# The third expert's first layer by seven half products, in the last three token pairs instead of the last two

## The chip, the cores and the metric

The kernel runs on one NeuronCore of one Trainium2 chip. The metric is the device time of one execution in microseconds (us). Shorter is better.

## The reference

An attention stage (4 batches, 8 heads, 768 positions, head width 64; three heads attend to the whole past, five to four sink positions and a window of 64) gives `x`, 3072 tokens of 512 values. A mixture of four experts then works on every token:

```python
p = domain_probs / (domain_probs.sum(-1, keepdims=True) + 1e-09)
out = zeros((N, D))                      # N = 3072, D = 512
for e in range(4):
    h = maximum(x @ w1[e], 0.0)          # w1[e]: 512 x 1024
    out += p[:, e:e+1] * (h @ w2[e])     # w2[e]: 1024 x 512
```

The change is in the product `x @ w1[e]` of one expert, for 256 of the 3072 tokens.

## The kernel before, in words

**Stages.** The tokens are cut in 24 tiles of 128. Tiles 0 to 3 are done in a plain way. Tiles 4 to 23 are done two at a time: ten *pairs*, whose first tiles are 4, 6, ..., 18, 20, 22 (`pairs`; `nt0` is the first tile of a pair, `nxt` that of the following one). The attention of the later tokens is woven into the earlier pairs and has ended before pair 18 begins. From there only the mixture is left.

**A pair** (`pair_steps`) is a first layer for four experts, then one second layer over all four. The probability is multiplied into the inputs beforehand (`scale_inputs`, L1150, on VectorE), so the second layer can sum over the experts in PSUM. The hidden values go to `hA`, five blocks of 16 x 128 columns: A11, A21, A12, A22 and `S1 = A21 + A22`.

**A plain first layer** (`plain_layer1`, L1199) is four steps of eight matmuls with 256 columns each. Every step fills one of four PSUM banks of the pool `pA`, and ScalarE empties it with a ReLU (L1208).

**A first layer by seven half products** (`winograd_layer1`, L1228) cuts weights and inputs in 2 x 2 blocks and makes seven products instead of eight, each of eight matmuls with 128 columns. Call them 1 to 7. They use two banks, x and y, that accumulate:

- 1 goes into x; ScalarE copies x out (`keep`, L1238).
- 2 goes into a `pA` bank; VectorE adds the copy and clips (`add`, L1245).
- 3 is accumulated on x, and x is copied out.
- 4 goes into y, and y is copied out.
- 5 is accumulated on x; VectorE adds a copy and clips.
- 6 is accumulated on y; VectorE adds a copy and clips.
- 7 is accumulated on x; ScalarE reads x with a ReLU (L1278).

It needs sums of inputs (`scaled_sums`, L1166 and two `minus` at L992, then one `minus` inside step 4) and sums of weights, made once per expert (`first_weight_sums`: three new matrices `more[0]` to `more[2]`, and `more[3]`, which overwrites a quarter of `w1sb`).

**Which expert goes which way.** Expert 3 (`EW[0]`; its steps are called `a`) goes by half products in all pairs. Expert 2 (`EW[1]`, `b`) does so from pair 18 on (`two`). Expert 1 (`EW3`, `third`) does so in pairs 20 and 22 (`three`). Expert 0 is always plain (`n`). Where all three run, `b` has two banks of the pool `pV` for itself, with its own copies in `kS`, and `a` and `third` use the two banks of `pO` one after the other. The weight sums of expert 1 go to `vS`, the attention's room for values.

**The second layer** (`product`, L1361) is seven products of 16 matmuls with 256 columns, on the two `pO` banks again (`x`, `y`), with VectorE making S2, S3 and S4 between them (L992) and adding (L1384), and ScalarE copying (L1381). Beside it VectorE scales the inputs of the next pair.

**Order.** The order of all engines' instructions is written out by hand: in `pair_steps`, `order` is a list of (steps of TensorE work with what empties their banks, an operation placed after them). An engine works through its own list strictly in that order.

Of the kernel before, what the change touches and what calls it, by code (L numbers as in the profile page):

```python
# [19 lines left out]
def kernel(  # L20
# [80 lines left out]
    def bank():  # L101
        return pA.tile([P, 512], FP32, name="pA", bufs=4)
# [11 lines left out]
    EW = (E - 1, E - 2)  # L114
# [229 lines left out]
    def w1_tile(e, ct, ft):  # L344

        return w_tile(e, w1sb[:, e * DMP + ct, :], ft)
# [208 lines left out]
    def mm_ns(cols):  # L555
        return cols / 2.4 + 2.5
# [434 lines left out]
    def minus(out, a, b):  # L991
        nc.vector.tensor_tensor(out=out, in0=a, in1=b, op=ALU.subtract)  # L992
# [15 lines left out]
    def first_weight_sums(e):  # L1008

        return [  # L1010
            lambda: minus(t1[e, 0], w1_part(e, 0, 1), w1_part(e, 0, 0)),
            lambda: minus(t1[e, 1], w1_part(e, 1, 1), t1[e, 0]),
            lambda: minus(t1[e, 2], w1_part(e, 1, 0), t1[e, 1]),
            lambda: minus(w1_part(e, 0, 1), w1_part(e, 1, 1), w1_part(e, 0, 1)),
        ]

    def room_for_more_sums():

        x = kR[0].rearrange("p c n t x -> p (c n t x)")
        y = att.tile([P, KH * FN], FP16, name="t1", tag="k_rows", bufs=1)  # L1020
        for n in range(3):
            z = x[:, n * KH * FN : (n + 1) * KH * FN] if n < 2 else y
            t1[EW[1], n] = z.rearrange("p (c f) -> p c f", c=KH)
        x = att.tile([P, DMP * PC], FP16, name="xs1", tag="q16", bufs=1)
        own_room[EW[1]] = x.rearrange("p (c x) -> p c x", c=DMP)

    EW3 = E - 3

    def room_for_third():

        n = KH * FN
        for i in range(3):
            t1[EW3, i] = vSf[:, i * n : (i + 1) * n].rearrange("p (c f) -> p c f", c=KH)
# [90 lines left out]
    def load_probs(nt0):  # L1124
        pB_of[nt0] = moe.tile([P, PT, E, P], FP32, name="pB", tag="pB", bufs=1)
        rows = p_rows[nt0 : nt0 + PT, :]
        nc.sync.dma_start(
            out=pB_of[nt0].rearrange("p t e x -> p (t e x)"),
            in_=bass.AP(rows.tensor, rows.offset, [[0, P], [1, PT * E * P]]),
        )  # L1130

    def scaled(e):
        if e in own_room:
            return own_room[e]
        n = 2 if e == EW[0] else e % 2
        x = xs_of[0][:, n * DMP * PC : (n + 1) * DMP * PC]
        return x.rearrange("p (c x) -> p c x", c=DMP)

    def scale_inputs(nt0, e):

        if xs_of[0] is None:
            xs_of[0] = moe.tile([P, XS], FP16, name="xs", tag="xs", bufs=1)
        xs = scaled(e)
        for g, c0, t0, n in pieces(nt0):
            require(g)
            xin = xT[g][:, :, c0 : c0 + n * P].rearrange("p c (t x) -> p c t x", t=n)
            o = xs[:, :, t0 * P : (t0 + n) * P].rearrange("p c (t x) -> p c t x", t=n)
            pb = pB_of[nt0][:, t0 : t0 + n, e, :]
            pb = pb.rearrange("p t (c x) -> p c t x", c=1)
            nc.vector.tensor_tensor(  # L1150
                out=o, in0=xin, in1=pb.to_broadcast([P, DMP, n, P]), op=ALU.mult
            )

    def x_part(e, i, j):
        return scaled(e)[:, j * KH : (j + 1) * KH, i * P : (i + 1) * P]
# [3 lines left out]
    def x_sum(e, n):  # L1159

        n0 = (2 * P * 8 if e in second_set else WT * NSH * P) + n * KH * P
        return kSf[:, n0 : n0 + KH * P].rearrange("p (c x) -> p c x", c=KH)

    def scaled_sums(e):

        nc.vector.tensor_tensor(  # L1166
            out=x_sum(e, 0), in0=x_part(e, 1, 0), in1=x_part(e, 1, 1), op=ALU.add
        )
        minus(x_sum(e, 1), x_sum(e, 0), x_part(e, 0, 0))
        minus(x_part(e, 1, 0), x_part(e, 0, 0), x_part(e, 1, 0))  # L1170

    def first_sum(e, n=1):
        k = slice(e * HT, (e + n) * HT)
        nc.vector.tensor_tensor(
            out=S1[:, k, :], in0=A21[:, k, :], in1=A22[:, k, :], op=ALU.add
        )
# [8 lines left out]
    def two(nt0):  # L1185
        return nt0 >= pairs[-LAST]

    def three(nt0):
        return nt0 >= pairs[-2]

    def pair_steps(nt0, nxt):

        def plain_layer1(e):
            xs = scaled(e)
            for f0 in range(0, FTP, 2):
                ps = bank()
                for f in range(2):
                    for ct in range(DMP):
                        nc.tensor.matmul(  # L1199
                            out=ps[:, f * PC : (f + 1) * PC],  # L1200
                            lhsT=w1_tile(e, ct, f0 + f),
                            rhs=xs[:, ct, :],
                            start=(ct == 0),
                            stop=(ct == DMP - 1),
                        )
                b0 = 2 * (f0 // HT)
                k0 = e * HT + f0 % HT
                nc.scalar.activation(  # L1208
                    out=blocks[:, b0 : b0 + 2, k0 : k0 + 2, :].rearrange(
                        "p t f x -> p f t x"  # L1210
                    ),
                    in_=ps.rearrange("p (f t x) -> p f t x", f=2, t=2),
                    func=AF.Relu,
                )
                yield 2 * DMP * mm_ns(PC), 0.5
# [69 lines left out]
        a, b = (winograd_layer1(e, *y) for e, y in zip(EW, (banks, banks[::-1])))  # L1285
        if three(nt0):
# [5 lines left out]
            b = winograd_layer1(EW[1], *more_banks, more_kept)  # L1292
            third = winograd_layer1(EW3, *banks)

        more, last_more = [], None
        if nt0 == pairs[-LAST - 2]:
            room_for_more_sums()
            more = first_weight_sums(EW[1])
        elif nt0 == pairs[-LAST - 1]:
            last_more = first_weight_sums(EW[1])[3]  # L1300
        elif nt0 == pairs[-3]:
            room_for_third()
            more = first_weight_sums(EW3)
            last_more = more[3]
        if not two(nt0):
            n = itertools.chain(*(plain_layer1(e) for e in range(E - 1)))
            order = (
                ((n,), lambda: scale_inputs(nt0, 1)),
                ((n,), more[0] if more else None),
                ((n, a), lambda: last_weight_sum(E - 1) if nt0 == pair0 else None),  # L1310
                ((n, a), None),
                ((n, a), lambda: scale_inputs(nt0, 2)),
                ((n, a), lambda: load_probs(nxt)),
                ((n, a), more[1] if more else None),
                ((n, a), more[2] if more else None),
                ((n, a), lambda: first_sum(0, 2)),
                ((n,), None),
                ((n, n), lambda: first_sum(2, 2)),
                ((), lambda: scale_inputs(nxt, 1) if two(nxt) else None),
            )  # L1320
        elif three(nt0):
            n = plain_layer1(0)
            order = (
                ((), lambda: scaled_sums(EW[1])),
                ((a, b, a, b), lambda: load_probs(nxt) if nxt else None),
                ((a, b, a, b), None),
                ((a, b, a, b), None),
                ((a, b), lambda: scaled_sums(EW3)),
                ((n,), None),
                ((third, third, n), lambda: first_sum(EW[0])),  # L1330
                ((third, third, n), lambda: first_sum(EW[1])),
                ((third, third, n), lambda: first_sum(0)),
                ((third,), lambda: first_sum(EW3)),
            )
        else:
            n = itertools.chain(plain_layer1(0), plain_layer1(1))
            order = (
                ((a, a, n), more[0] if more else None),
                ((a, a, n), lambda: load_probs(nxt) if nxt else None),
                ((a, a, n), more[1] if more else None),  # L1340
                ((n,), lambda: scaled_sums(EW[1])),
                ((a, b, n), more[2] if more else None),
                ((b, b, n), lambda: first_sum(0)),
                ((b, b, n), lambda: first_sum(EW[0])),
                ((b, n, b), lambda: (first_sum(1), first_sum(EW[1]))),
            )
        for steps, op in order:
            for x in steps:
# [56 lines left out]

        last = nxt is None
        ahead = nxt and two(nxt)
        if ahead and three(nxt):
            inputs_for_third()
        half = KT // 2 * mm_ns(HN), PSHARE  # L1410
        yield from product(x, A11, b(0, 0), True)
# [62 lines left out]
    pairs = list(range(pair0, NTILE, PT))  # L1474
# [145 lines left out]
```

The softmax here doesn't subtract the row's maximum and nothing guards it: scores larger than these inputs give would overflow.

## Time and profile before

| what | value |
|---|---|
| time, median of 3 runs | 376.77 us (376.42 to 377.32) |
| the profiled execution, its own time | 376.68 us |
| span of the profiled execution | 375.0 us |
| TensorE busy | 367.9 us (98%) |
| VectorE busy | 279.0 us (74%) |
| ScalarE busy | 227.4 us (61%) |
| clock granted to TensorE | full in all slices |

The span runs from the first to the last instruction. The time has 1.7 us around it. In the trace, pair 18 runs from 296.10 us to 321.56 us, pair 20 from 321.56 us to 346.66 us, and pair 22 after it. PE is TensorE's matmuls, PEld its weight loads, DVE VectorE, ACT ScalarE, POOL GpSimd, SP SyncE. A line such as L1228 is that of kernel.py.

### The profile page before, as it was taken

How to read it: one execution, taken by the hardware profiler on the slowest of the kernel's cores; microseconds unless marked ns; L12 is line 12 of the kernel's file. 1: busy time of each engine (PE TensorE's matmuls, PEld its weight loads, DVE VectorE, ACT ScalarE, POOL GpSimd, SP SyncE). 2: the span in 40 equal slices, each digit the busy share in tenths (PEclk: the TensorE clock that was granted, in tenths of full speed). 3: DMA queues.
4: the chain of work that ended last, by engine and by line, in shares of the span. 5: the costliest groups of instructions: out<-in, count | busy, mean ns of one | idle time of the engine just before them, and what ended most of it. 6: DMA issues, size and time to landing. Idle time of an engine off the chain costs nothing.

```text
span 375.0 us, 10225 instructions
## 1 busy us (share of the span) xinstructions
PE 367.9 (98%) x4176; PEld 311.1 (83%) x4176; DVE 279.0 (74%) x599; ACT 227.4 (61%) x475; POOL 113.3 (30%) x155
## 2 busy tenths in 40 slices
PE   8899999999999999999999999999999999999996
PEld 5755466668998988999989898998899998998996
DVE  7774768697788669868658858957767968969762
ACT  3863478547785785765676955784778362450630
POOL 8924673982058038115601650320000000000000
PEclk9999999999999999999999999999999999999999
DMA  8999999999699569977904990951220300300101
GB/s 161 155 204 208 195 189 192 186 207 100 97 109 149 101 94 116 163 112 56 207 14 60 171 159 14 133 127 14 67 73 3 98 18 0 114 2 2 58 3 56
DMA packets 123747, 39.24 MB, mean 105 GB/s; under 512 B 113728, under 2 KB 116356, under 8 KB 123700
## 3 DMA queue, kind: packets, MB, share of 16 engines
q0 software_dynamic: 85824, 19.01, 58.7%
q1 hardware_dynamic: 36276, 19.18, 21.8%
q8 instruction: 32, 0.52, 0.6%
q10 hardware_dynamic: 1600, 0.39, 0.5%
q14 instruction: 15, 0.12, 0.1%
HBM read 44.89 MB, written 6.34 MB: 137 GB/s over the span
## 4 chain that ended last, share of the span: by engine, by line
PE 95%; DVE 2%; ACT 2%; issue 0%; ACTq 0%
PE pO L1361 31%; PE pA L1199 23%; PE pO L1228 9%; PE pA L1065 7%; PE pO L1086 7%; PE pA L678 5%; PE pV L734 2%; PE pV L806 2%; PE pA L1228 2%; PE pV L1228 1%; PE pO L448 1%; PE pA L576 1%; ACT es L696 1%; DVE xs L1150 1%; PE pA L1453 0%; ACT rc L824 0%
## 5 line engine op out<-in xcount | busy, mean ns | idle before, releaser
L1361 PEld LDWEIGHTS <-hA 128*128 128x128 f16 x1104 | 104.9, 98 | 12.3
L1199 PE MATMUL pA<-xs,w1sb 128*128 128x256 f16 x800 | 101.3, 273 | 0.0
L1199 PEld LDWEIGHTS <-w1sb 128*128 128x128 f16 x800 | 74.7, 98 | 7.9
L1208 ACT ACTIVATE hA<-pA 128x512 f16<-128x512 f32 x100 | 59.6, 598 | 31.2 <-PE pA L1199 29.0
L1361 PE MATMUL pO<-w2sb,hA 128*128 128x256 f16 x640 | 76.7, 272 | 0.0
L696 ACT ACTIVATE es<-pA 128x384 f16<-128x384 f32 (+2 forms) x122 | 59.2, 511 | 26.9 <-PE pA L678 23.0
L306 POOL DMA_DIRECT2D vS<-in_v_dram x30 | 29.6, 987 | 112.0 <-PE pV L806 111.0
L1361 PE MATMUL pO<-tsb,hA 128*128 128x256 f16 x464 | 56.7, 272 | 0.0
L1150 DVE TENSOR_TENSOR xs<-xT,pB 128x1024 f16<-128x1024 f16 (+1 forms) x49 | 47.0, 977 | 0.0
L992 DVE TENSOR_TENSOR hA<-hA 128x1024 f16<-128x1024 f16 x60 | 39.5, 685 | 0.5
L1078 ACT ACTIVATE hA<-pA 128x384 f16<-128x384 f32 (+1 forms) x64 | 22.2, 385 | 19.4 <-PE pA L1065 19.2
L1065 PE MATMUL pA<-xT,w1sb 128*128 128x384 f16 (+1 forms) x256 | 30.9, 273 | 0.8 <-DMA w1sb<-in_moe_w_dram 0.5
L1086 PE MATMUL pO<-w2sb,hA 128*128 128x512 f16 x128 | 30.7, 379 | 0.0
L1228 PEld LDWEIGHTS <-w1sb 128*128 128x128 f16 x480 | 29.6, 98 | 1.2 <-issue 0.2
L829 DVE TENSOR_TENSOR xT<-pV,rc 64x384 f16<-64x384 f32 x37 | 20.5, 554 | 11.8 <-ACT rc L834 9.4
L1381 ACT COPY s<-pO 128x256 f32<-128x256 f32 x31 | 11.5, 373 | 27.7 <-PE pO L1361 21.9
L1065 PEld LDWEIGHTS <-w1sb 128*128 128x128 f16 x256 | 19.4, 98 | 9.7 <-issue 1.4
L824 ACT ACTIVATE rc<-pV,eps 64x384 f32<-64x384 f32 x37 | 21.3, 576 | 6.5 <-PE pV L806 5.9
L700 DVE TENSOR_TENSOR es<-es,mS 128x384 f16<-128x384 f16 (+1 forms) x40 | 13.7, 344 | 15.0 <-ACT es L696 15.0
L1245 DVE CUSTOM_DVE_ANT_0 hA<-pO,s 128x512 f16<-128x512 f32 x26 | 17.6, 688 | 9.7 <-PE pO L1228 8.3
L1238 ACT COPY s<-pO 128x512 f32<-128x512 f32 x39 | 22.5, 587 | 2.3 <-PE pO L1228 2.0
L678 PE MATMUL pA<-qT,kR 128*128 128x384 f16 (+2 forms) x120 | 22.9, 278 | 0.4 <-DVE kR L595 0.2
(163 smaller groups left out, 515.6 us busy)
## 6 DMA issues: line engine op xcount, KB each, us to landing
pB<-p_rows SPq DMA_DIRECT2D x10, 512.0 KB
out_dram<-o SPq DMA_DIRECT2D x19, 256.0 KB
w1sb<-in_moe_w_dram POOLq DMA_DIRECT2D x8, 512.0 KB, 9.1
w2sb<-in_moe_w_dram POOLq DMA_DIRECT2D x4, 1024.0 KB, 12.4
vS<-in_v_dram POOLq DMA_DIRECT2D x30, 112.0 KB, 4.3
k_rows<-in_k_dram POOLq DMA_DIRECT2D x18, 128.0 KB, 5.5
q<-in_q_dram POOLq DMA_DIRECT2D x18, 128.0 KB, 7.0
vR<-in_v_dram POOLq DMA_DIRECT2D x24, 48.0 KB, 5.8
```

Of the source, the lines that this page charges most:

```text
L306: gp.dma_start(out=t[:, :, own_v(h)], in_=windows_of(v, b, h, c))
L678: nc.tensor.matmul(out=ps[:, o : o + nq], lhsT=key_tile(b, c, h, t), rhs=qTs[b, c][:, hp, q0 : q0 + nq], start=(n == 0 or not first), stop ...
L696: nc.scalar.activation(out=es[:, 0:cols], in_=ps[:, 0:cols], func=AF.Exp, scale=SC)
L992: nc.vector.tensor_tensor(out=out, in0=a, in1=b, op=ALU.subtract)
L1065: nc.tensor.matmul(out=pss[ft][:, 0:cols_n], lhsT=w1_tile(e, ct, ft), rhs=x[:, ct, :], start=(n == 0), stop=(n == DMP - 1),)
L1086: nc.tensor.matmul(out=ps_o, lhsT=hs[:, ft, j * P : (j + 1) * P], rhs=w2sb[:, e * FTP + ft, :], start=(ft == 0), stop=(ft == FTP - 1),)
L1150: nc.vector.tensor_tensor(out=o, in0=xin, in1=pb.to_broadcast([P, DMP, n, P]), op=ALU.mult)
L1199: nc.tensor.matmul(out=ps[:, f * PC : (f + 1) * PC], lhsT=w1_tile(e, ct, f0 + f), rhs=xs[:, ct, :], start=(ct == 0), stop=(ct == DMP - 1),)
L1208: nc.scalar.activation(out=blocks[:, b0 : b0 + 2, k0 : k0 + 2, :].rearrange("p t f x -> p f t x"), in_=ps.rearrange("p (f t x) -> p f t x" ...
L1228: nc.tensor.matmul(out=ps[:, f * P : (f + 1) * P], lhsT=w_tile(e, w[:, ct, :], f), rhs=a[:, ct, :], start=(first and f == 0 and ct == 0), ...
L1238: nc.scalar.copy(out=kept[n], in_=ps)
L1361: nc.tensor.matmul(out=ps, lhsT=a[:, k, :], rhs=b(k), start=(first and k == 0), stop=(k == KT - 1), skip_group_check=not first,)
```

## The change

In pair 18 expert 1 is done by seven half products too, in place of four plain steps. Its weight sums, which pair 18 made for the pairs after it, are now all made within pair 18's first layer; `more[3]` moves there from the end of the pair. Pair 18 takes over the arrangement of pairs 20 and 22 (`b` on `pV`, `third` on `pO` after `a`), with an order of its own.

```diff
     def three(nt0):
-        return nt0 >= pairs[-2]
+        return nt0 >= pairs[-3]
...
         elif nt0 == pairs[-3]:
             room_for_third()
             more = first_weight_sums(EW3)
-            last_more = more[3]
...
+        elif nt0 == pairs[-3]:
+            n = plain_layer1(0)
+            order = (
+                ((a, a, n), lambda: scaled_sums(EW[1])),
+                ((b, b, n), more[0]),
+                ((a, b, a, b), more[1]),
+                ((a, b, a, b), more[2]),
+                ((n, a, b), lambda: (scaled_sums(EW3), load_probs(nxt))),
+                ((third, third, n), more[3]),
+                ((third, third), lambda: first_sum(EW[0])),
+                ((third, third), lambda: first_sum(EW[1])),
+                ((third,), lambda: (first_sum(0), first_sum(EW3))),
+            )
         elif three(nt0):
             n = plain_layer1(0)
             order = (
...
                 ((third, third, n), lambda: first_sum(EW[0])),
                 ((third, third, n), lambda: first_sum(EW[1])),
                 ((third, third, n), lambda: first_sum(0)),
                 ((third,), lambda: first_sum(EW3)),
             )
-        else:
-            n = itertools.chain(plain_layer1(0), plain_layer1(1))
-            order = (
-                ((a, a, n), more[0] if more else None),
-                ((a, a, n), lambda: load_probs(nxt) if nxt else None),
-                ((a, a, n), more[1] if more else None),
-                ((n,), lambda: scaled_sums(EW[1])),
-                ((a, b, n), more[2] if more else None),
-                ((b, b, n), lambda: first_sum(0)),
-                ((b, b, n), lambda: first_sum(EW[0])),
-                ((b, n, b), lambda: (first_sum(1), first_sum(EW[1]))),
-            )
...
-        if ahead and three(nxt):
+        if ahead and three(nt0):
             inputs_for_third()
```

The last edit keeps `inputs_for_third` where it was: at the second layers of pairs 18 and 20.

## The prediction

> **What bounds the kernel now.** I read the busy table first, then the chain that ended last, then the stage of the change.
>
> ```profile
> PE 367.9 (98%) x4176; PEld 311.1 (83%) x4176; DVE 279.0 (74%) x599; ACT 227.4 (61%) x475; POOL 113.3 (30%) x155
> ...
> PE 95%; DVE 2%; ACT 2%; issue 0%; ACTq 0%
> ```
>
> TensorE is the bound: 98% busy, and 95% of the chain. What counts is matmul time and any gap that opens between matmuls. The view of busy time by stage, for the two layers of pair 18 and of pair 20, shows no gap there at all (the first PE number is busy time, to be held against the length before it):
>
> ```profile
> 296.10:309.34 13.24, 13.24 (x178) 12.51 (x177) 9.21 (x18) 8.38 (x16) 0.00 (x0) 1.00 0.28 82
> 309.34:321.56 12.22, 12.22 (x115) 10.96 (x113) 10.56 (x22) 1.96 (x5) 0.00 (x0) 1.00 0.01 1
> 321.56:334.44 12.88, 12.88 (x203) 12.51 (x201) 9.60 (x23) 8.08 (x16) 0.00 (x0) 1.00 0.25 83
> ```
>
> Pair 20's first layer already does what pair 18's is to do, and takes 12.88 us against 13.24. But it does so in another order. How its last half products are spaced is seen in the timeline of PE (start, length, what):
>
> ```profile
> 326.92 0.61 PE L1228 MATMUL pO<-xs,t1sb 128*128 128x128 f16 x8
> 327.37 0.61 PE L1228 MATMUL pV<-xs,t 128*128 128x128 f16 x8
> 327.82 1.04 PE L1199 MATMUL pA<-xs,w1sb 128*128 128x256 f16 x8
> 328.69 0.61 PE L1228 MATMUL pO<-vS,w1sb 128*128 128x128 f16 x8
> ...
> 330.46 1.06 PE L1228 MATMUL pO<-kS,vS 128*128 128x128 f16 x16
> 331.35 1.04 PE L1199 MATMUL pA<-xs,w1sb 128*128 128x256 f16 x8
> 332.22 1.06 PE L1228 MATMUL pO<-vS,w1sb 128*128 128x128 f16 x16
> 333.12 1.04 PE L1199 MATMUL pA<-xs,w1sb 128*128 128x256 f16 x8
> 333.99 0.61 PE L1228 MATMUL pO<-vS 128*128 128x128 f16 x8
> 334.44 3.66 PE L1361 MATMUL pO<-w2sb,hA 128*128 128x256 f16 x32
> ```
>
> Start to start, a half product takes 0.447 us and a plain step 0.873 us. A plain step stands between a7 and third 1 (call them t1 to t7), between t3 and t5, and between t5 and t7. These are pairs that share a PSUM bank, so the one must be read out before the other accumulates. How long that takes, the timelines of ACT and DVE in the same stretch say:
>
> ```profile
> 327.57 0.60 ACT L1278 ACTIVATE hA<-pO 128x512 f16<-128x512 f32 x1 [1.52 <-PE pO L1228]
> 331.15 1.07 ACT L1238 COPY s<-pO 128x512 f32<-128x512 f32 x2
> ```
>
> ```profile
> 332.97 1.29 DVE L1245 CUSTOM_DVE_ANT_0 hA<-pO,s 128x512 f16<-128x512 f32 x2 [1.40 <-PE pO L1228]
> ```
>
> ACT starts on t3's bank 0.69 us after t3's start (331.15 - 330.46) and takes 0.59 (two take 1.07, so the next may start 0.48 later). DVE starts on t5's bank 0.75 us after t5's start and takes 0.69 (two take 1.29, a pitch of 0.60). How fast TensorE follows a release shows in two places:
>
> ```profile
> 17.95 0.69 ACT L696 ACTIVATE es<-pA 128x256 f16<-128x256 f32 x2
> ...
> 18.36 0.11 PEld L734 LDWEIGHTS <-es 128*128 128x128 f16 x2 [1.15 <-ACT es L696]
> ```
>
> ```profile
> 345.98 1.21 DVE L1150 TENSOR_TENSOR xs<-xT,pB 128x1024 f16<-128x1024 f16 x1
> ...
> 347.25 0.61 PE L1228 MATMUL pV<-xs,w1sb 128*128 128x128 f16 x8
> ```
>
> The first activation (0.38) ends at 18.33 and the load starts at 18.36; the scaling ends at 347.19 and the matmul starts at 347.25. I take 0.06 us.
>
> So from a product to the next on its bank at least 0.69 + 0.59 + 0.06 = **1.34 us** pass by way of ACT, and 0.75 + 0.69 + 0.06 = **1.50 us** by way of DVE. Two half products fill 0.89 us; two and a plain step fill 1.77 us.
>
> **What the Trainium skill says.** "PSUM — Partial Sum Buffer", section "PSUM bank collisions raise a hardware error": TensorE's write and another engine's read of one bank must be kept apart in time, and the hardware does not stall by itself. So the waits are there in the program; the trace agrees in that no product starts before its bank's reader has ended. "TensorE: Matmul & The Clock Gate", section "The mechanism" (packing): matmuls start and end strictly in program order, so a waiting product holds up everything behind it; the trace shows them in order. The same page, "Back-to-back issue gap", gives about 81 ns for each matmul of 128 columns with its weight load; here it is 0.447 / 8 = 56 ns, and the trace decides.
>
> **The change part by part.**
>
> *Matmuls.* Out go four plain steps, 4 x 0.873 = 3.49 us; in come seven half products, 7 x 0.447 = 3.13. Gain **0.36 us**, the same as 13.24 - 12.88. In the built kernel TensorE has 24 matmuls and 24 weight loads more (56 for 32), as it should. ACT has 16 emptyings either way.
>
> *The order.* The plain steps that kept bank sharers apart are now fewer: four, spent after a2, b2, b6 and t2. The rest is back to back. I lay the new order on the old start, 296.10. Until b7 nothing waits: a3 to b6 alternate on four banks, 1.79 us from a product to the next on its bank, and a7 and b7 have a plain step more. Then:
>
> - b7 starts at 304.53, after a7 at 304.08. t1 accumulates in a7's bank. ACT reaches a7's ReLU at 304.77 (0.49 behind that of the plain step before it), ends at 305.36; t1 starts at 305.42 where 304.98 was possible: **0.44**.
> - t2 at 305.87, plain step at 306.32, t3 at 307.19, t4 at 307.64. ACT copies t3's bank from 307.88 to 308.47; t5 starts at 308.53 where 308.08 was possible: **0.45**.
> - t4's copy ends at 308.95; t6 starts at 309.01 for 308.98: **0.03**.
> - DVE adds t5's bank from 309.28 to 309.97; t7 starts at 310.03 for 309.46: **0.57**.
> - The second layer's first product takes t6's bank, by the wait of the built kernel. DVE adds it from 309.88 to 310.57; the product starts at 310.63 for 310.48: **0.15**.
>
> Sum 1.64 us of waiting; the layer lasts 14.5 us instead of 13.24.
>
> *VectorE's additions.* Three adds at 0.60, three input sums (0.74), one `minus` (0.21) and `more[3]` (0.60) come into this layer: 9.21 + 3.35 = 12.6 us of 14.5. It has idle places before a5's add, t2's add and t5's add, so its queue doesn't build up. By the same reckoning `more[3]` ends at 308.0, half a microsecond before t5 needs it, and t4's `minus` at 308.2 for t6 at 309.01. Cost nothing, covered by the wait for t5; if that cover goes, up to 0.5. `scaled_sums` for expert 2 moves ahead and ends at 299.03 for b3 at 300.07; the scaling before it ends at 297.18 for b1 at 297.86. Nothing.
>
> *What leaves the end of the pair.* `more[3]` (0.68 us at 322.15) stood in DVE's list behind the last scaling; pair 20 doesn't wait for it. Nothing.
>
> *Rooms and queues.* The attention's last use of `pV` ends at 291.5 us, of `kS` and `vS` before it: no wait. SP's and POOL's lists are the same in the built kernel; the load of probabilities waits for the last scaling of this pair (it issued at 297.21) as before. The second layer's own sums start at the same distance from its first product as now, since that product sets them off: it moves as a whole.
>
> Sum: -0.36 + 1.64 = **+1.28 us**. Against the profiled execution's own time, 376.68 + 1.28 = 377.96; it lies 0.09 under the median of three, 376.77. I say **378.0 us**. Unknown sizes: each of the four waits by 0.1 either way, and VectorE by 0 to 0.5.
>
> **Rivals.**
>
> *Banks come free early (not slower).* If the wait is satisfied while the reader is still at work, the waits vanish and the 0.36 us remain: 376.3. For all four to vanish ACT would have to free a bank 0.2 us after it begins (0.89 - 0.69). The two releases shown above, both at the record's end, speak against it. If only the DVE ones vanish, 377.2.
>
> *VectorE becomes the bound.* 12.6 of 14.5 us with waits in a fixed order leaves little. From the point where `more[3]` ends over 0.5 us later than reckoned, t5 waits for it, and the adds behind it shift too; a delay of 0.6 to 1.0 us beyond that point gives 378.6 to 379.0. For it speaks VectorE's unbroken run from 313.43 to 322 in the second layer, against it the idle places named.
>
> *The change doesn't do what it says.* The built instruction lists show that it does.
>
> **How the numbers follow.** About 0.2%, 0.75 us, is what a measurement of this kernel can tell from no change. The waits as reckoned: 0.76, own range 377.4 to 378.5. VectorE: 0.13. Early banks, whole or in part: 0.11. The range reaches from 376.9 to 379.0. Slower by over 0.2% needs 377.5: nearly all of the second case and some 85% of the first, together 0.78; within 0.2%: the rest of the first and most of the third, 0.19; faster: 0.03, since the matmuls saved are only 0.1%.
>
> **What would show it.** In the profile after, PE of pair 18's first layer is busy about 12.9 of 14.5 us, with gaps of 0.4 to 0.6 us ahead of t1, t5 and t7, released by ACT L1278, ACT L1238 and DVE L1245. It is wrong if that layer lasts under 13.3 us, or if a gap stands ahead of b1, b3 or pair 20.

## The result and the profile after

| | before | changed |
|---|---|---|
| median of 20 runs | 376.82 us | 377.91 us |
| ratio of the changed kernel to the one before | | 1.0034, 95% interval 1.0022 to 1.0045 |
| profiled execution, own time (span) | 376.68 us (375.0) | 377.64 us (375.9) |
| pair 18: first layer | 13.24 us | 14.49 us |
| pair 18: second layer | 12.22 us | 12.22 us |
| pair 20: first layer | 12.88 us | 12.88 us |

The changed kernel is slower by 1.28 us by the ratio (0.0034 x 376.82), with 0.8 to 1.7 in the interval; the medians differ by 1.09. In the profile pair 18's first layer is 1.25 us longer and nothing behind it has changed its length. The two spans differ by only 0.9, since in this execution pair 18 began at 295.72 us and not at 296.10; that difference of 0.38 is there by 42 us, in work that the change doesn't touch (0.21 of it by 21 us, where the first plain layer begins).

The busy table and the chain that ended last, of the changed kernel:

```profile
PE 367.6 (98%) x4200; PEld 311.0 (83%) x4200; DVE 282.1 (75%) x606; ACT 227.0 (60%) x475; POOL 113.2 (30%) x155
...
PE 94%; DVE 2%; ACT 2%; issue 1%; ACTq 0%; DVEq 0%
```

TensorE has 24 matmuls more, as it should. That it is busy 0.3 us less isn't the change's doing: up to 42 us, in work that the change doesn't touch, it is busy 0.57 us less (37.66 for 38.23), and in pair 18's first layer it is busy longer than before. The chain has lost a per cent of TensorE. Where it went is in busy time by stage (length of the stage from its bounds, then PE, PEld, DVE, ACT and POOL busy; the 1.00 behind them is the granted clock, full in every stage):

```profile
295.72:310.21 14.49, 13.55 (x201) 12.74 (x200) 12.22 (x26) 8.30 (x16) 0.00 (x0) 1.00 0.20 75
310.21:322.43 12.22, 12.22 (x113) 10.96 (x112) 10.85 (x23) 1.71 (x4) 0.00 (x0) 1.00 0.00 1
322.43:335.31 12.88, 12.88 (x203) 12.51 (x201) 9.17 (x22) 8.08 (x16) 0.00 (x0) 1.00 0.25 83
```

In the first of these stages, pair 18's first layer, PE is busy for less than the stage's length (13.55 of 14.49 us); before the change it was busy for all of it. The timeline of PE shows where; in brackets is the idle time and what ended it:

```profile
303.70 0.61 PE L1228 MATMUL pO<-xs,t1sb 128*128 128x128 f16 x8
304.14 0.61 PE L1228 MATMUL pV<-xs,t 128*128 128x128 f16 x8
305.03 0.61 PE L1228 MATMUL pO<-xs,w1sb 128*128 128x128 f16 x8 [0.28 <-ACT hA L1278]
...
306.80 1.06 PE L1228 MATMUL pO<-kS,vS 128*128 128x128 f16 x16
308.12 1.10 PE L1228 MATMUL pO<-xs,w1sb 128*128 128x128 f16 x16 [0.27 <-ACT s L1238]
309.61 0.61 PE L1228 MATMUL pO<-xs,vS 128*128 128x128 f16 x8 [0.39 <-DVE hA L1245]
310.21 3.65 PE L1361 MATMUL pO<-w2sb,hA 128*128 128x256 f16 x32
```

These are a7, b7, t1; then t3 with t4, t5 with t6, t7, and the second layer. Start to start a half product takes 0.447, so t1 was possible at 304.59 and came 0.44 later. In the same way t5 lost 0.43, t6 and t7 together 0.60 (0.04 of it ahead of t6: t5 with t6 takes 1.10 where t3 with t4 takes 1.06), and the second layer 0.15: **1.62 us**, and with the 0.37 us saved (13.24 - 12.87), 1.25. The figures in brackets are smaller because a group's length runs to the modelled end of its last matmul, some 0.16 us after the next one could start; the loss of 0.15 ahead of the second layer doesn't show as idle time at all. The time lost has to be read from start to start.

The readers that ended the waits, from the timelines of ACT and DVE of the changed kernel:

```profile
304.39 0.59 ACT L1278 ACTIVATE hA<-pO 128x512 f16<-128x512 f32 x1
307.49 1.07 ACT L1238 COPY s<-pO 128x512 f32<-128x512 f32 x2
```

```profile
306.96 0.68 DVE L992 TENSOR_TENSOR w1sb<-w1sb 128x1024 f16<-128x1024 f16 x1
...
308.87 1.29 DVE L1245 CUSTOM_DVE_ANT_0 hA<-pO,s 128x512 f16<-128x512 f32 x2 [0.69 <-PE pO L1228]
```

The ReLU of a7 ends at 304.98 and t1 starts at 305.03. The copy of t3 ends at 308.08 (307.49 + 0.59) and t5 starts at 308.12. The add of t5 ends at 309.56 or so (308.87 + 0.69) and t7 starts at 309.61. The add of t6 ends at 310.16 (308.87 + 1.29) and the second layer starts at 310.21; its first product reads A11, which t6 doesn't write, and t7's bank is still being read until 310.85, so what it takes over from t6 is the bank. Each time TensorE follows within 0.05 us. `more[3]`, the last weight sum, ends at 307.64, well before t5. VectorE itself stands idle for 0.69 us just before t5's add: it waits for TensorE, which has waited for ScalarE.

### The profile page after: what moved, and what is told of

Same layout as the page of the kernel before. It is cut to its first block, busy times and chain, and to the rows that moved or that the text cites. A ratio compares the mean times of both kernels' runs of the same rounds, so it can differ in the third digit from the quotient of the medians.

```text
span 375.9 us, 10284 instructions
## 1 busy us (share of the span) xinstructions
PE 367.6 (98%) x4200; PEld 311.0 (83%) x4200; DVE 282.1 (75%) x606; ACT 227.0 (60%) x475; POOL 113.2 (30%) x155
## 4 chain that ended last, share of the span: by engine, by line
PE 94%; DVE 2%; ACT 2%; issue 1%; ACTq 0%; DVEq 0%
PE pO L1361 31%; PE pA L1199 22%; PE pO L1228 9%; PE pA L1065 7%; PE pO L1086 7%; PE pA L678 5%; PE pV L1228 2%; PE pV L734 2%; PE pA L1228 2%; PE pV L806 2%; PE pO L448 1%; PE pA L576 1%; ACT es L696 1%; DVE xs L1150 1%; PE pA L1453 0%
## 5 line engine op out<-in xcount | busy, mean ns | idle before, releaser
L1199 PE MATMUL pA<-xs,w1sb 128*128 128x256 f16 x768 | 97.3, 272 | 0.0
L1199 PEld LDWEIGHTS <-w1sb 128*128 128x128 f16 x768 | 71.7, 98 | 7.6
L1208 ACT ACTIVATE hA<-pA 128x512 f16<-128x512 f32 x96 | 57.2, 597 | 31.0 <-PE pA L1199 28.8
L1228 PEld LDWEIGHTS <-w1sb 128*128 128x128 f16 x512 | 31.4, 98 | 1.9 <-issue 0.9
L1065 PEld LDWEIGHTS <-w1sb 128*128 128x128 f16 x256 | 19.3, 98 | 9.8 <-issue 1.4
```

The lines of the kernel that those rows point to most:

```text
L1065: nc.tensor.matmul(out=pss[ft][:, 0:cols_n], lhsT=w1_tile(e, ct, ft), rhs=x[:, ct, :], start=(n == 0), stop=(n == DMP - 1),)
L1199: nc.tensor.matmul(out=ps[:, f * PC : (f + 1) * PC], lhsT=w1_tile(e, ct, f0 + f), rhs=xs[:, ct, :], start=(ct == 0), stop=(ct == DMP - 1),)
L1208: nc.scalar.activation(out=blocks[:, b0 : b0 + 2, k0 : k0 + 2, :].rearrange("p t f x -> p f t x"), in_=ps.rearrange("p (f t x) -> p f t x" ...
L1228: nc.tensor.matmul(out=ps[:, f * P : (f + 1) * P], lhsT=w_tile(e, w[:, ct, :], f), rhs=a[:, ct, :], start=(first and f == 0 and ct == 0), ...
```

## The experiments

The theory on trial is that of **banks**: each gap is the time in which a reader empties the bank that the next product needs, left bare by the order. The rival is **VectorE**: it has three adds, three input sums, a `minus` and a weight sum more in this layer, 12.22 us of work, and what it makes comes late. All changes below are to pair 18 of the changed kernel alone; ratios are to the kernel before, where the changed kernel has 1.0034. The intervals of the ratios are 0.3 to 0.6 us wide on either side, too wide for most of the differences that are forecast; the length of the first layer in the trace decides. Such lengths repeat well: the second layer of pair 18 lasts 12.22 or 12.23 us in the traces of all eight kernels.

**Another bank, the same order.**

```diff
-            third = winograd_layer1(EW3, *banks)
+            third = winograd_layer1(EW3, *(banks[::-1] if nt0 == pairs[-3] else banks))
```

> Expert 1's two banks in pair 18 change places: its first product goes into the bank that a6 left, not into the one a7 just filled; the order of all work stays. Bank theory: the gap ahead of t1 (0.44 us) goes, the gaps ahead of t5 (0.43), t7 (0.56) and the second layer (0.15) stay; pair 18's first layer 14.05 us instead of 14.49, time 0.44 below the changed kernel, 0.8 above the kernel before. Order theory without banks (TensorE waits for ACT's ReLU because it is the a7-to-t1 place): no change. VectorE theory (its adds and sums are what is late): less than 0.2 gained, the rest comes back ahead of t5.

Measured: 377.53 us (ratio 1.0016, 1.0008 to 1.0024); the first layer takes 14.05 us, from 296.09 to 310.14. Timeline of PE:

```profile
304.51 0.61 PE L1228 MATMUL pV<-xs,t 128*128 128x128 f16 x8
304.96 0.61 PE L1228 MATMUL pO<-xs,w1sb 128*128 128x128 f16 x8
...
308.05 1.10 PE L1228 MATMUL pO<-xs,w1sb 128*128 128x128 f16 x16 [0.27 <-ACT s L1238]
309.54 0.61 PE L1228 MATMUL pO<-xs,vS 128*128 128x128 f16 x8 [0.40 <-DVE hA L1245]
```

t1 now follows b7 by 0.45 us, with no wait, though not one instruction has moved. The other gaps are as they were. What t1 had waited for is the bank, not the place in the order nor VectorE.

**A plain step over the first gap.**

```diff
-                ((n, a, b), lambda: (scaled_sums(EW3), load_probs(nxt))),
+                ((a, b, n), lambda: (scaled_sums(EW3), load_probs(nxt))),
```

> The plain step that stood ahead of a7 and b7 stands behind them. Bank theory: a plain step covers ACT's reading of a7's bank, so the gap ahead of t1 (0.44 us) goes and nothing else; a7, now 0.87 us earlier, has its bank back 0.3 us before it needs it. First layer 14.05 us, time 0.44 below the changed kernel. VectorE theory: less than 0.2 gained, with gaps ahead of a7 or t5 in its place.

Measured: 377.41 us (1.0017, 1.0008 to 1.0026); first layer 14.05 us, from 296.46 to 310.51. Timeline of PE:

```profile
303.11 0.61 PE L1228 MATMUL pV<-xs,w1sb 128*128 128x128 f16 x8
303.56 0.61 PE L1228 MATMUL pO<-xs,t1sb 128*128 128x128 f16 x8
304.01 0.61 PE L1228 MATMUL pV<-xs,t 128*128 128x128 f16 x8
304.45 1.04 PE L1199 MATMUL pA<-xs,w1sb 128*128 128x256 f16 x8
305.33 0.61 PE L1228 MATMUL pO<-xs,w1sb 128*128 128x128 f16 x8
```

The plain step fills the time of the ReLU. The same 0.44 us goes, here without a change of bank, and no gap opens ahead of a7 (303.56, 0.45 us after b6).

**The last plain step moved from behind t2 to behind t6.**

```diff
-                ((third, third, n), more[3]),
+                ((third, third), more[3]),
                 ((third, third), lambda: first_sum(EW[0])),
-                ((third, third), lambda: first_sum(EW[1])),
+                ((third, third, n), lambda: first_sum(EW[1])),
```

> The last plain step moves from behind t2 to behind t6. Bank theory: the gaps ahead of t7 (0.56 us) and the second layer (0.15) go, and one of 0.43 opens ahead of t3, which now has only t2 between itself and t1; t5's stays: first layer 14.22 us, time 0.27 below the changed kernel. VectorE theory: as more[3] then ends just when t5 wants it (307.64 for 307.68), t5's gap grows by up to 0.5, and nothing is gained.

Measured: 377.67 us (1.0016, 1.0008 to 1.0025); first layer 14.21 us, from 295.78 to 309.99. Timeline of PE:

```profile
305.54 0.61 PE L1228 MATMUL pA<-xs,w1sb 128*128 128x128 f16 x8
306.43 1.05 PE L1228 MATMUL pO<-kS,vS 128*128 128x128 f16 x16 [0.28 <-ACT s L1238]
307.76 1.07 PE L1228 MATMUL pO<-xs,w1sb 128*128 128x128 f16 x16 [0.28 <-DVE w1sb L992]
308.67 1.04 PE L1199 MATMUL pA<-xs,w1sb 128*128 128x256 f16 x8
309.54 0.61 PE L1228 MATMUL pO<-xs,vS 128*128 128x128 f16 x8
```

Timelines of ACT and of DVE:

```profile
307.07 1.07 ACT L1238 COPY s<-pO 128x512 f32<-128x512 f32 x2 [0.69 <-PE pO L1228]
```

```profile
307.02 0.68 DVE L992 TENSOR_TENSOR w1sb<-w1sb 128x1024 f16<-128x1024 f16 x1
```

The gaps ahead of t7 and of the second layer have gone, and one of 0.44 us has opened ahead of t3 (306.43 for 305.99). A plain step doesn't remove a wait in general: it removes the one it stands in. Ahead of t5 VectorE's weight sum (it ends at 307.70) has come up level with ScalarE's copy (307.66) and is now named as the one that ended the wait. By the release of 0.05 us seen above the copy alone would have let t5 start at 307.71; it started at 307.76, so VectorE cost some 0.05 us: its room is used up here. From t3 to t5 that makes 1.33 us, for 1.32 in the changed kernel, since ScalarE began its copy 0.64 us after t3 and not 0.69. In the changed kernel the ReLU of the plain step ahead of t3 stood before that copy in ScalarE's list (it begins at 307.00, and the copy 0.49 later), so some 0.05 us of the gap ahead of t5 seems to have been ScalarE's own queue; no run tests that by itself. The change of the time is within the noise of these medians; the layer's length decides.

**Without the weight sums.**

```diff
-                ((b, b, n), more[0]),
-                ((a, b, a, b), more[1]),
-                ((a, b, a, b), more[2]),
+                ((b, b, n), None),
+                ((a, b, a, b), None),
+                ((a, b, a, b), None),
...
-                ((third, third, n), more[3]),
+                ((third, third, n), None),
```

> The changed kernel without expert 1's four weight sums in pair 18 (left out of the computation): 2.4 us of VectorE work less in its first layer. Bank theory: all four gaps stay, time as the changed kernel within 0.1 us. VectorE theory: the gaps ahead of t5 and t7 shrink, 0.3 us and more gained.

Measured: 378.00 us (1.0032, 1.0021 to 1.0043), beside 377.09 of the kernel before on that chip. Busy time by stage:

```profile
296.00:310.49 14.49, 13.55 (x201) 12.70 (x201) 9.80 (x22) 8.30 (x16) 0.00 (x0) 1.00 0.22 75
```

VectorE has 2.4 us less to do (9.80 for 12.22) and the layer lasts 14.49 us to the hundredth. Ahead of t5's add VectorE now stands idle for 1.29 us where it was 0.69, waiting for TensorE. The weight sums cost nothing in the changed kernel, and VectorE isn't late there.

**One weight sum twice, at the place with the least room.**

```diff
-                ((third, third, n), more[3]),
+                ((third, third, n), lambda: (more[2](), more[3]())),
```

> The changed kernel with one weight sum made a second time just ahead of more[3] in pair 18: 0.60 us more of VectorE work at the place with the least room. more[3] ended at 307.64 in the profile of the changed kernel and t5 began at 308.12; bank theory: t5 waits for more[3] now, from 308.24 plus 0.06, so 0.18 us longer, and t6, t7 and the second layer move with it: time 0.18 above the changed kernel. VectorE theory (already the bound there): 0.6 above. If VectorE had a microsecond of room: no change.

Measured: 378.36 us (1.0041, 1.0026 to 1.0056); first layer 14.68 us, from 296.79 to 311.47. Timelines of DVE and of PE:

```profile
308.03 0.68 DVE L992 TENSOR_TENSOR vS<-w1sb,vS 128x1024 f16<-128x1024 f16 x1
308.63 0.68 DVE L992 TENSOR_TENSOR w1sb<-w1sb 128x1024 f16<-128x1024 f16 x1
```

```profile
307.87 1.06 PE L1228 MATMUL pO<-kS,vS 128*128 128x128 f16 x16
309.37 1.07 PE L1228 MATMUL pO<-xs,w1sb 128*128 128x128 f16 x16 [0.44 <-DVE w1sb L992]
```

`more[3]` ends at 309.31 now and t5 starts 0.06 later, released by it. It comes 1.50 us after t3, for 1.32 in the changed kernel: of 0.60 us put in, 0.18 came out, so VectorE had 0.42 us of room there, and no more. The layer is 0.19 longer (14.68 - 14.49).

**All waits covered by another order.**

```diff
-                ((b, b, n), more[0]),
-                ((a, b, a, b), more[1]),
-                ((a, b, a, b), more[2]),
-                ((n, a, b), lambda: (scaled_sums(EW3), load_probs(nxt))),
-                ((third, third, n), more[3]),
-                ((third, third), lambda: first_sum(EW[0])),
-                ((third, third), lambda: first_sum(EW[1])),
-                ((third,), lambda: (first_sum(0), first_sum(EW3))),
+                ((a, b), more[0]),
+                ((a, b), None),
+                ((a, b), more[1]),
+                ((a, b), more[2]),
+                ((a, b), lambda: scaled_sums(EW3)),
+                ((n, third, b), more[3]),
+                ((third, b), lambda: load_probs(nxt)),
+                ((third, third, n), lambda: first_sum(EW[0])),
+                ((third, third, n), lambda: (first_sum(EW[1]), first_sum(0))),
+                ((third,), lambda: first_sum(EW3)),
```

> A new order for pair 18: expert 2's steps begin two half products later and run between those of experts 3 and 1, and three of the four plain steps stand between t-steps that share a bank, so that three half products or more, or a plain step and more, lie between any two that share one. Bank theory: no gap is left; first layer 12.88 us, time 0.36 below the kernel before and 1.6 below the changed kernel (376.4 to 376.5). VectorE theory: it has the same work in 1.6 us less, so gaps of 0.3 us and more stay, ahead of b7, t5 or t7; time at or above the kernel before.

Measured: 376.49 us beside 376.87 of the kernel before on the same chip (ratio 0.9989, 0.9979 to 0.9999). Busy time by stage, and the end of the layer in the timeline of PE:

```profile
296.69:309.56 12.87, 12.87 (x200) 12.51 (x200) 12.16 (x26) 8.19 (x16) 0.00 (x0) 1.00 0.22 85
```

```profile
305.58 1.06 PE L1228 MATMUL pO<-kS,vS 128*128 128x128 f16 x16
306.47 1.04 PE L1199 MATMUL pA<-xs,w1sb 128*128 128x256 f16 x8
307.35 1.06 PE L1228 MATMUL pO<-xs,w1sb 128*128 128x128 f16 x16
308.24 1.04 PE L1199 MATMUL pA<-xs,w1sb 128*128 128x256 f16 x8
309.11 0.61 PE L1228 MATMUL pO<-xs,vS 128*128 128x128 f16 x8
```

The layer is as long as its matmuls, 12.87 us, with VectorE busy 12.16 us of it: 94%, and still not late. The same computation on the same banks takes 1.62 us less in this order. This kernel is faster than both others; against the one before by 0.1%, at the edge of what these runs can tell, while the layer's length (12.87 for 13.24) leaves no doubt.

## Why the prediction was right

It said 378.0 (377.96 by its sum). The median is 377.91, and the ratio gives 378.05 on the median shown before the change (376.77). The mechanism was the one forecast, and the sum was not right by errors that cancel: every term of it came out within 0.02 us. Step by step:

- *Matmuls, -0.36.* Measured 12.87 for 13.24 where nothing waits (the woven order).
- *Wait ahead of t1, 0.44.* Measured 0.44; shown to be the bank by the exchange of banks, and to be covered by a plain step.
- *Ahead of t5, 0.45, t6 and t7, 0.60, the second layer, 0.15.* Measured 0.43, 0.60 and 0.15. Here no bank was exchanged; for t5 to t7 it can't be, as these products accumulate on what the bank holds. That the wait is for its reader is shown by the times of release, by the plain step that took away the gaps ahead of t7 and of the second layer, by the woven order, which left none, and by the run without the weight sums, where they stayed as they were.
- *Release taken as 0.06 us.* Measured 0.04 to 0.05 behind ACT and DVE in the changed kernel, 0.06 behind the weight sum.
- *VectorE's additions cost nothing, with half a microsecond of room.* Measured: none without the sums, 0.42 us of room by the doubled one. The load that had looked close to a bound, 84% of the layer (12.22 of 14.49) and 94% in the woven order, was not one, because its idle places lie where it waits for TensorE. What the prediction added, up to 0.5 us more where the wait for t5 no longer covers the last weight sum, the woven order doesn't test: it makes that sum earlier (it ends at 306.36, a microsecond ahead of t5 at 307.35).
- *The second layer moves as a whole, pair 20 doesn't notice.* Measured 12.22 and 12.88 us, as before.

Some things were off in what the profile would look like. Busy time of PE was foreseen as 12.9 of 14.5 us and reads 13.55, and the idle times read 0.27 to 0.39 in place of 0.4 to 0.6: the prediction forgot that busy time counts each interrupted stream to its modelled end. VectorE's work in the layer was put at 12.6 us and reads 12.22, since one of the sums S1 (L1174, 0.42 us) that lay in the layer now falls behind it. And the layer's lengths differ by 1.25 where the sum gave 1.28.

The rival of early release fell with the first profile: no product started before its bank's reader ended. The rival of VectorE fell with the weight sums left out. That it would begin to count 0.5 us further on was close: it did so at 0.42.

## What to carry to other kernels

A saving in matmuls on a saturated TensorE is worth its size only if the new order keeps the distance between products that share a PSUM bank; here that distance was 1.32 us by way of ScalarE (some 0.05 of it, it seems, in ScalarE's own queue) and 1.49 by way of VectorE, and the steps that stood closer cost 1.62 us where 0.37 were saved. Before taking out filler work, list for each bank who writes it next and what lies between. When an arrangement is copied from another place (here from pairs 20 and 22), copy the order that covers its waits with it, or find one that does.

## What the runs showed of the hardware that was not expected

Little: TensorE takes up work 0.04 to 0.06 us after a reader's recorded end, with no further loss when a stream of matmuls starts again (half products after a wait keep 0.447 us start to start), and VectorE at 94% of a layer's length didn't hold TensorE up at all.
